# S4D convolution and gated GLU on one core: stores and small scale steps move from ScalarE and VectorE to GpSimd, and the last output stores are cut differently

## The chip, the cores and the metric

The program runs on one core of a Trainium2 chip. The metric is device time in microseconds; lower is better. The engines are called as the profile calls them: PE is TensorE, PEld its weight load, DVE VectorE, ACT ScalarE, POOL GpSimd, and SP SyncE, which only issues DMAs here. A name with a q behind it (ACTq, SPq) is that engine's sequencer, on whose rows the DMA issues of ACT and SP stand.

## What is computed

The input is u, 2048 tokens of 448 channels. With xn the layer norm of u over the channels:

```
out = u + S4D(xn) + GLU(xn)
S4D:  K[d, l] = 2 Re sum_n C[d, n] dt[d] exp(A[d, n] dt[d] l),   256 states n for each of 448 channels d
      y = irfft(rfft(xn, 4096) * rfft(K, 4096))[:2048] + xn * D_skip
GLU:  (sigmoid(xn @ w_gate) * (xn @ w_up)) @ w_down,   448 -> 1792 -> 448
```

All of it is in float32.

## The kernel before

Two generators are interleaved by weights written into the code: `conv()` makes the S4D kernel and the convolution, and `glu()` the gated products. A scheduler then orders each engine's instructions by its own model of the machine, with some priorities and orderings given by hand. Within an engine that order is fixed, and each instruction waits for its operands and its buffers.

**Tokens.** The 2048 tokens are 16 blocks of 128. The first half of the GLU works on blocks 0 to 7 and the second on blocks 8 to 15, each in two tiles of 512 tokens. A product in float32 is made of three matmuls of rounded parts (high times high, low times high, high times low), so weights and activations stand twice, as `wh` and `wl`, `hh` and `hl`, `dh` and `dl`. The gate and up products are L709, the down products L825; DVE adds the latter into `acc` (L830). GpSimd makes `dl` (L786) for the first half.

**Norm.** `x_stats` (L245) gives mean and variance of a block, and `x_scales` (L250) the factor `ys` and the offset `zs` by three Newton steps from an integer guess, on DVE, for four blocks at a time in the first half and for all eight of the second half at once. `x_norm` applies them; for the second half that happens late, at about 270 us.

**First stage of x's transform.** For each pair of blocks, PE multiplies by a table `wx` (L280), ACT copies the result out of PSUM, and it is stored to `x1_d` in DRAM. For the first half `x_spec` (L282) does this at about 41 to 73 us: four calls, each with two of three tiles `x1a`, `x1b`, `x1c` in turn (the trace writes `x1ab` for the first two), PSUM banks `tr`, `ko` and `kp`, copies at L293 and L295, and four stores at L300, issued by ACT. A tile can be written again only when its stores have landed, and a bank only when its copy is done. For the second half `pair_first` (L681) does it at about 273 to 330 us: four calls with four PSUM banks `gu`, copies at L689 and four stores at L691, also issued by ACT. Nothing reads `x1_d` before the spectra, after 510 us.

**S4D kernel.** From about 107 to 510 us GpSimd builds magnitudes `me` and `mf` (L508, L520) for two groups of channels at a time, one pair ahead; DVE multiplies them into `Et` and `Ft` (L602 to L604), and PE sums them (`ko`, L616). GpSimd also adds the skip to `ks` (L627) and, from 332 us, issues loads of weights for the second half (L640 to L648).

**End.** The spectra's last inverse stage (L962) is done in steps `last(h, m)` that add into `acc` tiles for channel half h; those for h = 1 stand between the last four down products (L811 to L818). `out` (L235) stores blocks of tokens in four DMAs, one for each group of 32 partitions. The first channel half of blocks 8 to 11 goes on POOL's queue; the rest of blocks 8 to 11, then blocks 12 to 14, then block 15 go on the queues of SP and ACT in turn.

Of the kernel before, what the change touches and what calls it, by code (L numbers as in the profile page):

```python
# [15 lines left out]
ALU = mybir.AluOpType  # L16
# [4 lines left out]
D = 448  # L21
# [18 lines left out]
H = D // 2  # L40
# [91 lines left out]
def s4d_glu_kernel(ctx, tc, io):  # L132
    nc = tc.nc
    hp = tc.high_priority
    v = nc.vector
# [114 lines left out]
    def x_scales(sm, b0, nb):  # L250

        st6, mv, ve, z = sm
        y = ys[:, b0 : b0 + nb]
        b = slice(b0 % 8, b0 % 8 + nb)
        v.tensor_scalar(ve[:, b], mv[:, b, 1], 1e-5, None, ALU.add)  # L255
        v.tensor_scalar(y.bitcast(I32), ve[:, b].bitcast(I32), -0.5, 1597463007.0, ALU.mult, ALU.add)
        for _ in range(3):
            v.tensor_tensor(z[:, b], y, y, ALU.mult)
            v.scalar_tensor_tensor(z[:, b], z[:, b], -0.5, ve[:, b], ALU.mult, ALU.mult)
            v.scalar_tensor_tensor(y, z[:, b], 1.5, y, ALU.add, ALU.mult)  # L260
        neg = lim[:, b0 // 4, 0:1] if b0 < 8 else -1.0
        v.scalar_tensor_tensor(zs[:, b0 : b0 + nb], mv[:, b, 0], neg, y, ALU.mult, ALU.mult)
        if b0 < 8:
            limits(b0 // 4)

    def x_norm(xn, xt, b):
        y_, z_ = ys[:, b : b + 1], zs[:, b : b + 1]
# [14 lines left out]
    def x_spec(xn, b0):  # L282

        x1s_ = []
        for _ in range(2):
            x1s_.append(slots[("x1a", "x1b", "x1c")[x1s[0] % 3]])
            x1s[0] += 1
        ps = psc[-1].tile([128, 2, 512], F32, name="tr", bufs=1)
        kk = [psc[-1].tile([128, 512], F32, name=n, bufs=1) for n in ("ko", "kp")]
        with tc.issue_after(glu_mm[0].ins):  # L290
            for j in range(4):
                x_first_stage((ps[:, j] if j < 2 else kk[j - 2])[:, :D], xn, j)
        nc.scalar.copy(x1s_[0], ps[:, :, :D])  # L293
        for j in range(2):
            nc.scalar.copy(x1s_[1][:, j], kk[j][:, :D])  # L295
        for p in range(2):
            r = row(b0, 2 * p)
            for h in range(2):
                to = x1_d[h].rearrange("(g r) k d -> g r k d", r=8)[r // 8 : r // 8 + 2, r % 8 : r % 8 + 2]
                nc.scalar.dma_start(to.rearrange("g i k d -> (i k) g d"), x1s_[p][:, :, H * h : H * h + H])  # L300
        yield 2 * WX

    def exp(ex, ki, fr, pl):
# [377 lines left out]
    def pair_first(b, xns):  # L681

        x1 = pg.tile([128, 2, D], F32, name="x1", tag="wraw", bufs=1)
        pss = [psg.tile([128, 512], F32, name="gu", bufs=4) for _ in range(4)]
        for g in range(4):
            x_first_stage(pss[g][:, :D], xns, g)
        for g in range(4):
            to = x1[:, g] if g < 2 else pg.tile([128, D], F32, name="x1", tag="rd", bufs=RB)
            nc.scalar.copy(to, pss[g][:, :D])  # L689
            r = row(b, g)  # L690
            nc.scalar.dma_start(  # L691
                x1_d[:, r : r + 2].rearrange("h i k d -> (i k) h d"), to.rearrange("p (h d) -> p h d", h=2)
            )

# [35 lines left out]
    def glu():  # L730
        for half in range(2):
# [4 lines left out]
            for fs_ in ORDER[half]:  # L736
# [68 lines left out]
                for t in range(2):  # L805
                    acc = accs[2 * half + t]
                    for b in range(4):
                        if final and (t, b) == (0, 1):

                            yield None  # L810
                        if final and t == 1 and b >= 2:  # L811

                            sp_mm[:] = glu_mm
                            for m in (4 * b - 8, 4 * b - 6):
                                lasts[0](1, m)
                            if b == 3:
                                out(accs[2], 8, 4, slice(H, D), (nc.sync, nc.scalar))
                                out(accs[3], 12, 3, slice(0, D), (nc.sync, nc.scalar))  # L818
                        po = psg.tile([128, D], F32, name="po", tag="gu", bufs=4)
                        bs = slice(128 * b, 128 * b + 128)  # L820
                        n = 0
                        with tc.issue_after(sp_mm[0].ins) if glu_on else nullcontext():
                            for (hh, hl), (dh, dl) in zip(hs[t], wts):
                                for a_, w_ in ((hh, dh), (hh, dl), (hl, dh)):
                                    glu_mm[:] = [nc.tensor.matmul(  # L825
                                        po, a_[:, bs], w_, start=(n == 0), stop=(n == 3 * fc - 1)
                                    )]
                                    n += 1
                        with hp(HP):
                            v.scalar_tensor_tensor(  # L830
                                acc[:, b], po, 0.5, acc[:, b], ALU.mult, ALU.add
                            )
                        yield 0.6 * fc
                        if cross and (t, b) in downs:
                            step(*downs[t, b])
# [2 lines left out]
                    if final and t == 0:  # L838
                        out(acc, 8, 4, slice(0, H), (nc.gpsimd,))
                    elif final:  # L840
                        out(acc, 15, 1, slice(0, D), (nc.sync, nc.scalar))

    def spectra(pf):

# [310 lines left out]
```

## Time and profile before

| | us |
|---|---|
| runs | 711.12, 714.69, 714.64 |
| median | 714.64 |
| profiled execution | 710.54 |
| its span, first to last instruction | 708.8 |
| PE busy | 668.1 |
| DVE busy | 555.7 |
| ACT busy | 428.7 |
| POOL busy | 384.9 |
| mean granted clock of TensorE | 0.988 |

The profile is of one execution, which was shorter than the median. DMA issues of ACT and SP are not counted as busy, those of POOL are shown as its own rows. A row of the timeline gives start and duration in us, engine, line, operation, the tiles written and read, and in brackets the idle time of the engine ahead of it with what ended it. Rows of windows give start and end of a stretch, then the busy time of each engine in it, the granted clock (1.00 is full), the share of the DMA engines and GB/s.

### The profile page before, as it was taken

The page shows a single profiled execution, that of the slowest core. Times are in us where ns is not written, and L with a number is a line of the kernel's source. Part 1 is how long each engine was busy: PE and PEld are TensorE (multiplying, and loading weights), DVE is VectorE, ACT ScalarE, POOL GpSimd, SP SyncE. Part 2 cuts the span into 40 slices and gives each one's busy share as a digit, 9 for nine tenths or more (in the row PEclk, how much of TensorE's full clock was granted, in tenths as well). Part 3 has the DMA queues.
Part 4 walks back from the last instruction along what each step waited for, and adds up shares of the span by engine and source line. Part 5 has one row for each costly group of instructions (what it writes and reads, how often), then busy time and mean ns, then how long its engine had stood idle before and what let it go on. Part 6 is the DMA issues. An engine that isn't in the chain of part 4 may idle for free. (4 is left out here: it accounts for less than half of the span.)

```text
span 708.8 us, 19098 instructions
## 1 busy us (share of the span) xinstructions
PE 668.1 (94%) x7752; PEld 523.7 (74%) x7752; DVE 555.7 (78%) x766; ACT 428.7 (60%) x678; POOL 384.9 (54%) x433
## 2 busy tenths in 40 slices
PE   2798999999999998999999999999999999999996
PEld 2575878878877875756878878877777777777784
DVE  5899987699899998898478899988946555566544
ACT  3656965578689779877577788778543322322320
POOL 2101227655999999777446698798765001344001
PEclk9999999999999998989999999999999999999999
DMA  9956274554253544546833333242269988999756
GB/s 200 239 149 204 70 230 150 170 183 132 63 169 135 169 123 135 162 146 202 258 112 103 92 112 108 68 138 82 54 179 280 257 236 238 266 272 221 182 146 182
DMA packets 93031, 117.22 MB, mean 165 GB/s; under 512 B 12240, under 2 KB 76624, under 8 KB 92944
## 3 DMA queue, kind: packets, MB, share of 16 engines
q1 hardware_dynamic: 65376, 91.75, 46.3%
q10 hardware_dynamic: 24896, 18.13, 8.7%
q0 software_dynamic: 2672, 6.13, 3.2%
q8 instruction: 61, 1.00, 0.6%
q14 instruction: 26, 0.21, 0.1%
HBM read 72.13 MB, written 43.84 MB: 164 GB/s over the span
## 5 line engine op out<-in xcount | busy, mean ns | idle before, releaser
L520 POOL TENSOR_TENSOR me<-me,pm 128x32 f32<-128x32 f32 (+1 forms) x168 | 154.9, 922 | 66.8 <-DVE Et L603 38.1
L520 POOL TENSOR_TENSOR mf<-mf,pm 128x64 f32<-128x64 f32 (+1 forms) x112 | 116.9, 1044 | 5.1
L709 PE MATMUL gu<-xh,wh 128*128 128x512 f32 x336 | 100.1, 405 | 3.8 <-DVE acc L830 1.6
L709 PE MATMUL gu<-xh,wl 128*128 128x512 f32 x336 | 96.9, 393 | 0.0
L709 PE MATMUL gu<-xl,wh 128*128 128x512 f32 x336 | 95.1, 390 | 0.0
L602 DVE TENSOR_TENSOR Et<-me,S 128x1024 f32<-128x1024 f32 x56 | 80.2, 1433 | 11.6 <-ACT S L551 10.3
L825 PE MATMUL po<-dh,hh 128*128 128x448 f32 x224 | 84.2, 376 | 3.1 <-ACT hh L725 1.9
L548 ACT ACTIVATE S<-tr 128x1024 f32<-128x1024 f32 x56 | 57.7, 1030 | 44.9 <-PE tr L542 41.0
L604 DVE TENSOR_TENSOR Ft<-mf,S 128x1024 f32<-128x1024 f32 x56 | 80.1, 1431 | 5.3 <-PE ko L616 3.7
L603 DVE TENSOR_TENSOR Et<-me,S 128x1024 f32<-128x1024 f32 x56 | 80.4, 1436 | 4.8 <-ACT me L533 4.5
L825 PE MATMUL po<-dh,hl 128*128 128x448 f32 x224 | 82.4, 369 | 0.3 <-DVE hl L727 0.3
L825 PE MATMUL po<-dl,hh 128*128 128x448 f32 x224 | 82.3, 368 | 0.0
L709 PEld LDWEIGHTS gu<-xh,wh 128*128 128x128 f32 x336 | 60.8, 189 | 24.2 <-issue 4.4
L709 PEld LDWEIGHTS gu<-xh,wl 128*128 128x128 f32 x336 | 63.4, 189 | 14.7 <-DVE ve L255 0.7
L709 PEld LDWEIGHTS gu<-xl,wh 128*128 128x128 f32 x336 | 63.0, 188 | 13.5
L725 ACT CAST hh<-hf 128x512 fp32r<-128x512 f32 x56 | 34.9, 623 | 62.4 <-DVE hf L720 61.4
L616 PEld LDWEIGHTS ko<-Et,Ft 128*32 128x32 f32 x3584 | 54.7, 112 | 24.2 <-issue 13.4
L720 DVE SCALAR_TENSOR_TENSOR hf<-th,gu 128x512 f32<-128x512 f32 x56 | 38.1, 680 | 39.9 <-PE gu L709 35.2
L786 POOL TENSOR_TENSOR dl<-rd,dh 128x448 fp32r<-128x448 f32 x14 | 25.6, 1830 | 78.8 <-ACT dh L785 68.5
L616 PE MATMUL ko<-Et,Ft 128*32 128x64 f32 x3584 | 65.2, 223 | 2.6 <-DVE Ft L604 2.4
L551 ACT ACTIVATE S<-S,hpi 128x1024 f32<-128x1024 f32 x56 | 65.5, 1170 | 0.0
L717 ACT ACTIVATE th<-gu 128x512 f32<-128x512 f32 x56 | 33.5, 599 | 49.4 <-PE gu L709 43.0
(208 smaller groups left out, 1318.0 us busy)
## 6 DMA issues: line engine op xcount, KB each, us to landing
sk_d<-sk ACTq DMA_DIRECT2D x14, 512.0 KB
sx<-x_d SPq DMA_DIRECT2D x32, 224.0 KB
skl<-sk_d SPq DMA_DIRECT2D x16, 448.0 KB
vp<-v_d SPq DMA_DIRECT2D x16, 448.0 KB
v_d<-vt SPq DMA_DIRECT2D x14, 448.0 KB
ph<-ph_d SPq DMA_DIRECT2D x224, 24.0 KB
wt_d<-wh SPq DMA_DIRECT2D x9, 512.0 KB
wt_d<-wl SPq DMA_DIRECT2D x9, 512.0 KB
```

The source lines that it names most:

```text
L520: ins = nc.gpsimd.tensor_tensor(m[:, :, w + a : 2 * w : n], m[:, :, a:w:n], par(base + i).unsqueeze(2).to_broadcast([128, 4 * DC, w // n]) ...
L548: nc.scalar.activation(rows(cs), pv, AF.Abs)
L551: sins[:] = [nc.scalar.activation(cs, cs, AF.Sin, scale=-TWO_PI, bias=hpi)]
L602: v.tensor_tensor(Et[:, :, :, 32:64], two(me[:, :, 32:64]), S[:, 1::-1], ALU.mult)
L603: v.tensor_tensor(Et[:, :, :, 0:32], two(me[:, :, 0:32]), S[:, 1:3, :, ::-1], ALU.mult)
L604: fts[:] = [v.tensor_tensor(Ft, two(mf), S[:, 3:5], ALU.mult)]
L616: mm = nc.tensor.matmul(ko[32 * j : 32 * j + 32, sl], Ft[:, cc, DC * h + 4 * q + j], Et[:, cc, DC * h + 4 * q + j], start=(k == 0), stop=( ...
L709: glu_mm[:] = [nc.tensor.matmul(ps, a_, b_, start=(n == 0), stop=(n == len(mm) - 1))]
L717: marks[0] = nc.scalar.activation(th, pgu[0], AF.Tanh, scale=0.5)
L720: marks[1] = v.scalar_tensor_tensor(hf, th, 1.0, pgu[1], ALU.add, ALU.mult)
L725: nc.scalar.copy(hh, hf)
L825: glu_mm[:] = [nc.tensor.matmul(po, a_[:, bs], w_, start=(n == 0), stop=(n == 3 * fc - 1))]
```

## The change

- The stores of `x_spec` and of `pair_first` are issued by GpSimd and no longer by ACT: 32 DMAs.
- For the second half (`b0 >= 8`) the three Newton steps and `zs` are computed by GpSimd, in 14 instructions of 128x8 in place of ten on DVE, since a step is made of four single operations.
- The last stores are cut differently: the first channel half of blocks 12 and 13 is stored from POOL's queue as soon as block 13's down product is added; at the end SP and ACT store the second channel half of blocks 8 to 11, that of blocks 12 and 13, and then blocks 14 and 15 whole.

```diff
@@ x_scales
+        if b0 >= 8:
+            for _ in range(3):
+                nc.gpsimd.tensor_tensor(z[:, b], y, y, ALU.mult)
+                nc.gpsimd.tensor_tensor(z[:, b], z[:, b], ve[:, b], ALU.mult)
+                nc.gpsimd.tensor_scalar(z[:, b], z[:, b], -0.5, 1.5, ALU.mult, ALU.add)
+                nc.gpsimd.tensor_tensor(y, y, z[:, b], ALU.mult)
+            nc.gpsimd.tensor_tensor(z[:, b], mv[:, b, 0], y, ALU.mult)
+            nc.gpsimd.tensor_scalar(zs[:, b0 : b0 + nb], z[:, b], -1.0, None, ALU.mult)
+            return
         for _ in range(3):
             v.tensor_tensor(z[:, b], y, y, ALU.mult)
             v.scalar_tensor_tensor(z[:, b], z[:, b], -0.5, ve[:, b], ALU.mult, ALU.mult)
             v.scalar_tensor_tensor(y, z[:, b], 1.5, y, ALU.add, ALU.mult)
@@ x_spec
-                nc.scalar.dma_start(to.rearrange("g i k d -> (i k) g d"), x1s_[p][:, :, H * h : H * h + H])
+                nc.gpsimd.dma_start(to.rearrange("g i k d -> (i k) g d"), x1s_[p][:, :, H * h : H * h + H])
@@ pair_first
-            nc.scalar.dma_start(
+            nc.gpsimd.dma_start(
                 x1_d[:, r : r + 2].rearrange("h i k d -> (i k) h d"), to.rearrange("p (h d) -> p h d", h=2)
             )
@@ glu, last down products
                             if b == 3:
                                 out(accs[2], 8, 4, slice(H, D), (nc.sync, nc.scalar))
-                                out(accs[3], 12, 3, slice(0, D), (nc.sync, nc.scalar))
+                                out(accs[3], 12, 2, slice(H, D), (nc.sync, nc.scalar))
...
+                        if final and (t, b) == (1, 1):
+                            out(acc, 12, 2, slice(0, H), (nc.gpsimd,))
...
                     elif final:
-                        out(acc, 15, 1, slice(0, D), (nc.sync, nc.scalar))
+                        out(acc, 14, 2, slice(0, D), (nc.sync, nc.scalar))
```

Since the scheduler orders each engine anew, the change moves instructions beyond those that it names. In the order of the changed program the line numbers are up to nine higher.

On POOL, in the stage of `x_spec`, before: `dl` is the low part of a weight tile of the down product, `pm` a tile of powers.

```order
L1064 DMA sel<-in_c_sel_dram 128x512
L786 TENSOR_TENSOR dl<-rd,dh 128x448 x2
L584 MEMSET pm_1167 128x128
L786 TENSOR_TENSOR dl<-rd,dh 128x448 x2
L477 MEMSET pm_1110 128x128
```

And after, from the same load of `sel` on, as far as the second store of the first `x1c`:

```order
L1073 DMA sel<-in_c_sel_dram 128x512
L793 TENSOR_TENSOR dl<-rd,dh 128x448
L307 DMA x_d<-x1ab 128x2x224 x4
L259 TENSOR_TENSOR z<-ys 128x8
L260 TENSOR_TENSOR z<-z,ve 128x8
L261 TENSOR_SCALAR z<-z 128x8
L262 TENSOR_TENSOR ys<-ys,z 128x8
...
L307 DMA x_d<-x1c 128x2x224 x2
L261 TENSOR_SCALAR z<-z 128x8
L307 DMA x_d<-x1ab 128x2x224 x2
L262 TENSOR_TENSOR ys<-ys,z 128x8
L793 TENSOR_TENSOR dl<-rd,dh 128x448
```

The rows left out are six more Newton rows, so ten stand ahead of the first stores of `x1c`; the last row is the `dl` that started at 54.69 us before, and two stores of `x1ab` and two more Newton rows stand ahead of it as well.

On ACT, in the same stage, before: copies out of PSUM for `x_spec`, stores, and the GLU's `hh`.

```order
L293 COPY x1c<-tr 128x896
L759 CAST wh<-wraw 128x1024
L295 COPY x1ab<-ko 128x448
L373 ACTIVATE s_381<-s_381 112x512
L300 DMA x_d<-x1c 128x2x224 x2
...
L295 COPY x1c<-ko 128x448
L300 DMA x_d<-x1ab 128x2x224 x2
L295 COPY x1c<-kp 128x448
L725 CAST hh<-hf 128x512
```

After:

```order
L300 COPY x1c<-tr 128x896
L766 CAST wh<-wraw 128x1024
L302 COPY x1ab<-ko 128x448
L380 ACTIVATE s_385<-s_385 112x512
...
L302 COPY x1c<-ko 128x448
L302 COPY x1c<-kp 128x448
L732 CAST hh<-hf 128x512
```

The copies keep their places, and the stores between them are gone; the second pair of copies to `x1c` and `hh` behind them now depend on stores in POOL's order.

On DVE, in the stage of `pair_first`, at about 306 to 311 us, before: `xl` is the low part of the normed tokens, read out of the bank that PE's next transposes need.

```order
L720 SCALAR_TENSOR_TENSOR hf<-th,gu 128x512
L269 TENSOR_SCALAR xt<-xt,ys,zs 128x448
L220 TENSOR_TENSOR xl<-gu,xh 128x2x256
L604 TENSOR_TENSOR Ft<-mf_1108,S_1103 128x1024
L454 SCALAR_TENSOR_TENSOR pm_1110<-pm_1110 128x128
L830 SCALAR_TENSOR_TENSOR acc<-po,acc 128x448
L223 TENSOR_TENSOR xl<-gu,xh 128x256
```

After:

```order
L727 SCALAR_TENSOR_TENSOR hf<-th,gu 128x512
L276 TENSOR_SCALAR xt<-xt,ys,zs 128x448
L220 TENSOR_TENSOR xl<-gu,xh 128x2x256
L611 TENSOR_TENSOR Ft<-mf_1112,S_1107 128x1024
L461 SCALAR_TENSOR_TENSOR pm_1114<-pm_1114 128x128
L223 TENSOR_TENSOR xl<-gu,xh 128x256
L837 SCALAR_TENSOR_TENSOR acc<-po,acc 128x448
```

`acc` and the second `xl` have changed places. In the same stage POOL's 16 stores stand among its magnitudes: four ahead of the second pair of groups in that stage, four ahead of the third, four within it or at its end, and four within the fourth, ahead of the loads of L640.

More of the change, by code (lines that the diff above doesn't have):

```diff
@@ L260, in x_scales @@
             v.scalar_tensor_tensor(y, z[:, b], 1.5, y, ALU.add, ALU.mult)
[L261 to L264, printed above, removed]
+        v.scalar_tensor_tensor(zs[:, b0 : b0 + nb], mv[:, b, 0], lim[:, b0 // 4, 0:1], y, ALU.mult, ALU.mult)
+        limits(b0 // 4)
     def x_norm(xn, xt, b):
```

## The prediction

> **What bounds the kernel now.** I read the busy shares and the clock row of the page first, then the chain that ended last, then what TensorE (PE) waited for, stage by stage.
>
> ```profile
> PE 668.1 (94%) x7752; PEld 523.7 (74%) x7752; DVE 555.7 (78%) x766; ACT 428.7 (60%) x678; POOL 384.9 (54%) x433
> ...
> PEclk9999999999999998989999999999999999999999
> ```
>
> PE is busy 94% of the span of 708.8 us, so some 41 us at most are not matmuls. ScalarE (ACT), from which work is taken, is busy only 60%. The clock row is full but for two slices at about 270 to 320 us. The chain of work that ended last shows the tail:
>
> ```profile
> 694.71 1.67 PE pv L962 x64
> ...
> 700.08 2.03 PE po L825 x9
> 702.10 0.02 issue
> 702.12 0.62 DVE acc L830
> ```
>
> The chain is PE almost throughout; the last sum of VectorE (DVE) ends at 702.74, and the remaining 6.06 us are output stores. Where PE did wait in the stages that the change touches, its timeline says (start, duration, what; in brackets the idle time ahead and its releaser):
>
> ```profile
> 61.25 0.47 PE L825 MATMUL po<-dh,hh 128*128 128x448 f32 x1 [1.85 <-ACT hh L725]
> ...
> 69.41 0.47 PE L825 MATMUL po<-dh,hh 128*128 128x448 f32 x1 [1.20 <-DVE acc L830]
> ...
> 305.91 1.99 PE L280 MATMUL gu<-xt,wx 32*64 32x448 f32 x8 [0.92 <-DVE hf L720]
> ...
> 309.89 0.56 PE L213 MATMUL gu<-ident,xt 128*64 128x128 f32 x2 [0.77 <-DVE xl L223]
> ```
>
> These waits name DVE, or ACT's hh that itself waited for DVE's hf (its row is below). No wait names an issue of a store. Behind the gaps near 270 to 310 us lies a second price, in the windows (length, then busy time and count of PE, PEld, DVE, ACT, POOL, then granted clock, DMA share, GB/s):
>
> ```profile
> 270.00:280.00 10.00, 8.00 (x96) 4.20 (x94) 10.00 (x12) 9.54 (x17) 9.61 (x9) 0.96 0.34 95
> 280.00:290.00 10.00, 10.00 (x150) 6.93 (x149) 6.28 (x7) 8.24 (x14) 8.67 (x12) 0.69 0.51 160
> 300.00:310.00 10.00, 8.26 (x120) 4.90 (x119) 9.52 (x13) 7.59 (x14) 9.28 (x13) 1.00 0.50 162
> 310.00:320.00 10.00, 10.00 (x122) 6.74 (x122) 9.61 (x11) 8.83 (x15) 4.96 (x6) 0.66 0.35 110
> ```
>
> After a window in which PE was busy 8.00 of 10 (and again 8.26), the granted clock falls: 0.04, 0.31 and 0.34 of 10 us are lost, 0.4 + 3.1 = 3.5 us and 3.4 us. So one such stretch is worth up to 3.5 us of PE.
>
> **The change part by part.**
>
> *Stores of the first stage leave ACT.* Sixteen are issued at 43 to 73 us and sixteen at 278 to 330 us. What one cost ACT is read from what ACT starts beside it:
>
> ```profile
> 43.22 0.40 ACTq L300 DMA_DIRECT2D x_d<-x1ab  x1
> 43.29 0.64 ACT L725 CAST hh<-hf 128x512 fp32r<-128x512 f32 x1
> ...
> 55.45 1.92 ACTq L300 DMA_DIRECT2D x_d<-x1ab  x2
> ...
> 57.41 0.53 ACT L295 COPY x1c<-kp 128x448 f32<-128x448 f32 x1 [1.56 <-PE gu L709]
> ...
> 60.58 0.62 ACT L725 CAST hh<-hf 128x512 fp32r<-128x512 f32 x1 [2.64 <-DVE hf L720]
> ...
> 301.98 2.77 ACTq L691 DMA_DIRECT2D x_d<-x  x2
> 304.79 0.58 ACT L219 CAST xh<-gu 128x512 fp32r<-128x512 f32 x1 [2.41 <-issue]
> ```
>
> hh starts 0.07 us after an issue of 0.40 began: an issue normally costs ACT nothing, since it runs beside computing. Twice it did not: ACT stood still for 1.56 us before 57.41 (the row names PE, but the gap ends with the issue, at 57.37) and for 2.41 us before 304.79. Both were covered: after the first, ACT waited another 2.64 us for hf; during the second DVE worked on. So 3.97 us of ACT go, and the path gets **0**; what is late next is DVE in both places.
>
> *The same stores on GpSimd (POOL).* The trace has no such store there; the nearest issues are these, with the landing times of the output stores:
>
> ```profile
> L239 POOL DMA_DIRECT2D out_dram<-ac x8 | 4.4, 554 | 0.1
> L640 POOL DMA_DIRECT2D wraw<-in_B_w_up_dram x5 | 3.9, 778 | 0.0
> ...
> DMA to landing us min/median/max: 2.4/2.7/6.9
> ```
>
> So 0.55 to 0.78 us each (the mean ns of the rows); a store of 128x2x224 lies between these shapes, and I take 0.6. In the second stage 16 x 0.6 = 9.6 us (8.8 to 12.5) come onto POOL in front of the magnitudes. The cover is POOL's own waiting for DVE to release a buffer of me:
>
> ```profile
> 292.64 6.69 POOL L520 TENSOR_TENSOR me<-me,pm 128x32 f32<-128x32 f32 x6 [3.73 <-DVE Et L603]
> ...
> 319.79 4.59 POOL L520 TENSOR_TENSOR me<-me,pm 128x32 f32<-128x32 f32 x6 [4.73 <-DVE Et L603]
> ```
>
> The order puts four stores ahead of the first wait (2.4 us against 3.73) and eight between the two (4.8 against 4.73): just covered, and the magnitudes are made one pair of groups ahead of their use. I take **0**; if the cover were gone, the end would slip by the excess, at most 12.5 - 8.46 = 4.0 us.
>
> *Newton steps.* Ten rows leave DVE. Their cost there is the spacing of starts:
>
> ```profile
> 47.38 0.17 DVE L256 TENSOR_SCALAR ys<-ve 128x8 int32<-128x8 int32 x1
> ...
> 53.54 0.16 DVE L258 TENSOR_TENSOR z<-ys 128x8 f32<-128x8 f32 x1
> 53.62 1.76 DVE L322 RECIPROCAL m<-m 112x128 f32<-112x128 f32 x2
> ...
> 68.74 0.62 DVE L830 SCALAR_TENSOR_TENSOR acc<-po,acc 128x448 f32<-128x448 f32 x1
> ```
>
> 53.62 - 53.54 = 0.08 us each, 0.8 in all; five stand ahead of the acc at 68.74 on which PE waits: 0.4 us earlier. On POOL they become 14 instructions. The nearest shape is ks (128x8), and beside it stands what POOL and DVE do to each other:
>
> ```profile
> L627 POOL TENSOR_TENSOR ks<-ks,dm x14: 215/654/1192, 163.5 to 524.8; 128x8 f32<-128x8 f32 x14
> ...
> 36.44 1.15 POOL L786 TENSOR_TENSOR dl<-rd,dh 128x448 fp32r<-128x448 f32 x1 [11.26 <-ACT dh L785]
> ...
> 84.11 4.41 POOL L786 TENSOR_TENSOR dl<-rd,dh 128x448 fp32r<-128x448 f32 x1 [24.74 <-ACT dh L785]
> ...
> 88.02 1.05 DVE L392 SCALAR_TENSOR_TENSOR w<-ci,w 112x512 f32<-112x512 f32 x1
> ```
>
> The same dl took 1.15 us at 36 us and 4.41 at 84 us, inside a dense run of DVE; at its end the DVE instruction at 88.02 took 1.05, where its neighbours start 0.60 apart: POOL waited for DVE, then DVE 0.4 for POOL. So the 14 steps cost POOL 3.0 to 16.7 us, 9.2 at the median, and give DVE back at least one such wait of 0.4 because dl moves behind them. I put the Newton part at -0.4 + 0.4 = **0** on the path, with -0.4 to +3 as its bounds (14 short waits of 0.2).
>
> Queued behind them are two stores of x1c, the third dl and the next stores; this is the wait that the change adds. Ten steps stand ahead of the x1c stores. From 47.55 (ys ready): 10 x 0.65 = 6.5, two issues 1.2, landing 2.7 give **57.95**; only then may ACT overwrite x1c (two copies, 1.1 us, before: 55.29 and 57.41) and go on to hh. That makes 59.05, ahead of the 60.58 at which hh starts anyway. Covered by 1.5 us.
>
> The Trainium skill, "SBUF — State Buffer", section "Who interferes with whom", says that a DVE instruction with two SBUF inputs and a GpSimd one that reads SBUF exclude each other for a whole instruction. The 4.41 us row agrees with it. By that rule alone the steps come late and in lumps, and the time is that of the second rival below; by the median of the ks row it is the sum's. The same page's section "SBUF: two separate sides" adds that GpSimd's own DMA descriptors can be locked out by some DVE modes; no row here shows that.
>
> *The tail.* The last stores, by queue (KB each):
>
> ```profile
> out_dram<-acc SPq DMA_DIRECT2D x2, 168.0 KB
> ...
> out_dram<-acc SPq DMA_DIRECT2D x2, 112.0 KB
> ...
> out_dram<-acc SPq DMA_DIRECT2D x2, 56.0 KB
> ...
> 703.00:704.00 1.00, 0.00 (x0) 0.00 (x0) 0.00 (x0) 0.00 (x0) 0.00 (x0) 1.00 1.05 325
> ```
>
> Before: 2 x (112 + 168 + 56) = 672 KB on SP's queue and as much on ACT's; after: 2 x (56 + 112 + 112) = 560. 224 KB leave the tail for POOL's queue, some 8 us earlier. After the last sum the DMA engines are full (share 1.05 at 325 GB/s), so the end follows the bytes: 224 / 325 = **0.7 us** less. The bounds are 0 (if the last 448 KB, now twice those before, set the end by their own issue) and -1.2 (if also 0.5 us of earlier start counts).
>
> *Sum.* 0 + 0 + 0 - 0.7 = -0.7 us. Against the profiled execution's own 710.54 us that is 709.8. That execution is 4.1 us under the median of the runs shown, 714.64; these lie at 711.12 and at 714.64 to 714.69, which is one clock stretch of 3.5 apart (an inference: only one run has a profile). The change decides nothing about that that I can price, so the forecast for the median is 714.64 - 0.7 = **713.9 us**.
>
> **The rivals.** *One clock stretch fewer.* In the order, xl now stands ahead of acc:
>
> ```profile
> 308.90 0.61 DVE L830 SCALAR_TENSOR_TENSOR acc<-po,acc 128x448 f32<-128x448 f32 x1
> 309.43 0.41 DVE L223 TENSOR_TENSOR xl<-gu,xh 128x256 fp32r<-128x256 f32 x1
> ```
>
> That takes 0.5 us of PE's 0.77 wait at 309.89, right ahead of the drop of the clock. If it is enough, 3.4 us go: 713.9 - 3.4 = **710.5**. Against it: the gaps at 273 to 278 us stay, and it is a threshold that I cannot see. The same time comes out if the median run just falls into the faster group.
>
> *The stores of x1c come late.* At 1.19 us a step, the most for that shape, ten steps end at 59.45, the stores are issued by 60.65 and land at 63.35; ACT's copies end at 64.45, hh at 65.1, and PE goes on at about 65.1 and not 61.25: 3.8 us, of which the later 1.2 us wait gives back that much: 2.6. A gap of PE of that length would bring a clock stretch of 3.4 too: 713.9 + 6.0 = **719.9**, slower than before. It decides from landings later than 59.5 us. For it speaks the 4.41 us row; against it that DVE's reciprocals at 53.6 to 57.5 have one input.
>
> **How the numbers follow.** A measurement of this kernel tells about 0.5% (3.6 us) from no change. Forecast 713.9, within 0.5%: 0.42. Fewer stretches, or the faster group, at 710.5 and faster by over 0.5%: 0.36. Late stores, or POOL's cover gone by the full 4.0 us with a stretch: 0.22. The range reaches from 709.0 (710.5 less the tail's other 0.5 and a further 1) to 718.0 (713.9 and the 4.0 us); left out is most of the late-store case.
>
> **What would show it.** In the changed profile: the ACT stalls at 55 and 302 us are gone and no PE wait with them; the x1c stores on POOL start before 55 us and ACT's second copy to x1c ends by 60.5; POOL's waits for Et shrink to near 0 but PE never names POOL's me; DMA is idle after the last sum 0.7 us sooner. I am wrong if PE waits longer than 2 us at 58 to 66 us, if the count of windows below full clock changes, or if the last store ends later against the last sum than the 6.06 us of before.

## The result, and the profile after

| | median, us | runs | ratio to before on the same chip | 95% interval |
|---|---|---|---|---|
| before | 712.79 | 5 | | |
| after | 723.13 | 5 | 1.0153 | 1.0124 to 1.0183 |
| after, measured once more beside the experiments | 726.50 | 5 | 1.0169 | 1.0148 to 1.0191 |

The forecast was 713.9 us, 709.0 to 718.0: no change. The kernel became 1.5 to 1.7% slower, 10 to 12 us. The profiled execution took 722.0 us, with a span of 720.2, against 710.54 and 708.8.

The page, read at the same two lines as before:

```profile
PE 675.9 (94%) x7752; PEld 529.3 (73%) x7752; DVE 560.7 (78%) x756; ACT 428.2 (59%) x678; POOL 415.6 (58%) x483
...
PEclk9999999999999999979899999999999999999999
```

The shares say almost nothing: PE is again at 94%, and POOL has 30.7 us more to do but is still idle 42% of the time. PE's waits say more (who waited for whom: total, times, longest). Before, the longest wait for Ft was 0.7 us:

```profile
PE ko L616 <- DVE Ft L604: 2.4, 5, 0.7
...
PE po L825 <- DVE acc L830: 1.2, 1, 1.2
```

After:

```profile
PE ko L623 <- DVE Ft L611: 10.2, 4, 6.7
PE po L832 <- DVE acc L837: 3.3, 1, 3.3
```

In PE's timeline after, the wait of 1.85 us at 61.25 is gone (between 58 and 70 us PE now waits at most 0.48). The wait of 1.20 us for acc at 69.41 has grown to 3.26, and the wait of 6.70 is new:

```profile
72.29 0.47 PE L832 MATMUL po<-dh,hh 128*128 128x448 f32 x1 [3.26 <-DVE acc L837]
...
359.19 1.93 PE L623 MATMUL ko<-Et,Ft 128*32 128x64 f32 x64 [6.70 <-DVE Ft L611]
```

The windows after show what lies behind such gaps:

```profile
310.00:320.00 10.00, 9.09 (x89) 4.46 (x86) 9.94 (x15) 6.94 (x13) 9.56 (x12) 0.58 0.36 114
...
350.00:360.00 10.00, 3.30 (x43) 2.52 (x46) 2.70 (x3) 1.45 (x2) 0.91 (x2) 0.80 0.77 247
360.00:370.00 10.00, 10.00 (x182) 7.99 (x178) 7.87 (x10) 5.32 (x9) 5.42 (x9) 0.86 0.53 136
```

The first row answers to before's 0.66 in the same window. From 350 to 370 us the clock was full before (1.00 in both windows). Now PE loses 6.70 us there to the wait and about 1.8 us to the clock behind it. The two windows together lose 0.20 + 0.14 of 10 us, 3.4 us of clock, but 1.6 of these fall into the wait itself, where PE had nothing to run: in windows of 2 us the clock is 0.51 from 356, 0.50 from 358 and from 360, and 0.79 from 362. Where the time goes is best read from one mark that both programs have in the same order, DVE's 56 instructions Ft. Their start after, less that before, in the profiled executions (us; the column heads are times of before):

```
                                   120.3  278.8  330.4  342.3  381.6  519.9  end of span
after                                2.5    4.1    4.2   15.6   12.5   12.5   11.4
after, second profile                3.4    5.5    5.2   15.6   13.2   13.3   13.2
before with the new tail only        0.3    0.2    2.8    2.8    2.9    3.1    6.5
```

There are two losses: 2.5 to 3.4 us before 120 us, and 8 us between 330 and 380 us. The last row is a warning: that program has the order of before up to its last stores, so its drift of 2.8 us at 320 us and of 3 more behind 520 us is the scatter between executions. Single traces show mechanisms; sizes are taken from the ratios of the runs.

**The loss in the middle is a chain over four queues.** After, on POOL: the last of `pair_first`'s stores stand between steps of `mf`.

```profile
336.06 3.44 POOL L527 TENSOR_TENSOR mf<-mf,pm 128x64 f32<-128x64 f32 x3
339.44 0.75 POOL L698 DMA_DIRECT2D x_d<-x  x1
340.21 1.08 POOL L527 TENSOR_TENSOR mf<-mf,pm 128x512 f32<-128x512 f32 x1
341.21 1.47 POOL L698 DMA_DIRECT2D x_d<-x  x2
```

On SP, after: the load of `t` (the spectra's table t32, not read before 510 us) reuses a tile that these stores read. It stood at the head of SP's queue, and what it waited for stands in SP's own waits:

```profile
SPq L986 <- DMA x_d<-x: 9.9, 1, 9.9
```

```profile
344.02 0.36 SPq L986 DMA_DIRECT2D t<-in_c_t_dram  x1
...
347.24 0.54 SPq L846 DMA_DIRECT2D acc_d<-acc  x1
347.87 8.95 SPq L499 DMA_DIRECT2D ph<-ph_d  x8
```

Before, the same rows of SP came some 10 us earlier, and the next phase loads 12.9 us behind the store:

```profile
333.17 0.36 SPq L977 DMA_DIRECT2D t<-in_c_t_dram  x1
...
337.75 0.38 SPq L837 DMA_DIRECT2D acc_d<-acc  x1
...
350.68 6.10 SPq L492 DMA_DIRECT2D ph<-ph_d  x8
```

The last sum for this store ended at 335.90 before and at 340.71 after. So of the 11.4 us by which the load of `acc` below starts later (344.86 and 356.24), 4.8 are lateness that the program already had, 4.7 were added by SP's queue ahead of the store, and 1.9 passed between the store and the load (7.1 us before, 9.0 after).

The store of `acc` (the finished sums of tokens 512 to 1023) must land before `acc`'s buffer is loaded anew, and that load is issued by ACT (L243). Here the scheduler's new order matters. On ACT before, the four loads followed `hh`; after, one of them stands ahead of it:

```profile
343.28 0.62 ACT L724 ACTIVATE th<-gu 128x512 f32<-128x512 f32 x1
356.24 0.32 ACTq L243 DMA_DIRECT2D acc<-in_A_u_dram  x1
356.65 0.62 ACT L732 CAST hh<-hf 128x512 fp32r<-128x512 f32 x1 [12.75 <-DMA ph<-ph_d]
```

ACT stood still for 12.75 us with `hf` ready since 345.45, and so did DVE, with `hl` and then `Ft` behind it:

```profile
344.76 0.69 DVE L727 SCALAR_TENSOR_TENSOR hf<-th,gu 128x512 f32<-128x512 f32 x1 [4.05 <-PE gu L716]
357.30 0.69 DVE L734 TENSOR_TENSOR hl<-hf,hh 128x512 fp32r<-128x512 f32 x1 [11.85 <-ACT hh L732]
357.91 1.22 DVE L611 TENSOR_TENSOR Ft<-mf,S 128x1024 f32<-128x1024 f32 x1
```

The row of `hh` names the phase loads, which share SP's queue with the store; that it is the store which ACT waits for is an inference from the buffer that the load writes, and the experiments below bear it out. Before, `hh` ran first and the loads could wait as long as they liked; the `th` behind them waited 5.75 us, with no wait of PE:

```profile
341.03 0.62 ACT L725 CAST hh<-hf 128x512 fp32r<-128x512 f32 x1 [1.03 <-DVE hf L720]
344.86 2.45 ACTq L243 DMA_DIRECT2D acc<-in_A_u_dram  x4
347.40 0.60 ACT L717 ACTIVATE th<-gu 128x512 f32<-128x512 f32 x1 [5.75 <-DMA acc<-in_A_u_dram]
```

**The early loss is a chain too.** Before, POOL made the third `dl` as soon as ACT had made `dh`, and the load of the next `rd` followed on SP:

```profile
54.69 2.23 POOL L786 TENSOR_TENSOR dl<-rd,dh 128x448 fp32r<-128x448 f32 x1 [17.09 <-ACT dh L785]
```

```profile
56.95 0.35 SPq L648 DMA_DIRECT2D rd<-in_B_w_down_dram  x1
```

After, twelve Newton instructions and eight stores stand on POOL between the second `dl` and the third:

```profile
48.00 0.65 POOL L259 TENSOR_TENSOR z<-ys 128x8 f32<-128x8 f32 x1
...
53.53 1.49 POOL L307 DMA_DIRECT2D x_d<-x1c  x2
...
58.50 1.58 POOL L793 TENSOR_TENSOR dl<-rd,dh 128x448 fp32r<-128x448 f32 x1
```

So `dl` began 3.8 us later. It frees the tile `rd`; the load of the next `rd` heads SP's queue and went out 3.2 us later, with the loads of `wraw` behind it. ACT's `wh` waits for these loads:

```profile
60.11 0.35 SPq L655 DMA_DIRECT2D rd<-in_B_w_down_dram  x1
```

```profile
68.80 1.04 ACT L766 CAST wh<-wraw 128x1024 fp32r<-128x1024 f32 x1 [2.05 <-DMA wraw<-in_B_w_up_dram]
```

The new order has this `wh` ahead of `hh` on ACT, and `wl` ahead of the `acc` on DVE that PE waited 3.26 us for. Before, `hh` stood first:

```profile
66.82 0.62 ACT L725 CAST hh<-hf 128x512 fp32r<-128x512 f32 x1
...
67.96 1.03 ACT L759 CAST wh<-wraw 128x1024 fp32r<-128x1024 f32 x1
```

### The profile page after: what moved, and what is told of

Same layout as the page of the kernel before. It is cut to its first block, busy times and chain, and to the rows that moved or that the text cites. A ratio compares the mean times of both kernels' runs of the same rounds, so it can differ in the third digit from the quotient of the medians.

```text
span 720.2 us, 19137 instructions
## 1 busy us (share of the span) xinstructions
PE 675.9 (94%) x7752; PEld 529.3 (73%) x7752; DVE 560.7 (78%) x756; ACT 428.2 (59%) x678; POOL 415.6 (58%) x483
## 4 chain that ended last, share of the span: by engine, by line
PE 68%; DVE 17%; DMA 5%; ACT 3%; issue 3%; SPq 3%; POOL 1%; ACTq 0%; DVEq 0%; POOLq 0%
PE gu L716 30%; PE po L832 14%; PE sp L911 7%; PE ko L623 5%; PE pv L938 4%; PE tr L549 3%; DVE Ft L611 3%; DVE Et L609 3%; DVE Et L610 2%; DMA acc<-in_A_u_dram 1%; DMA acc_d<-acc 1%; DVE acc L837 1%; PE pv L971 1%; SPq L649 1%; DVE hl L734 1%
## 5 line engine op out<-in xcount | busy, mean ns | idle before, releaser
L527 POOL TENSOR_TENSOR mf<-mf,pm 128x64 f32<-128x64 f32 (+1 forms) x112 | 114.0, 1018 | 5.1
L716 PE MATMUL gu<-xl,wh 128*128 128x512 f32 x336 | 96.6, 394 | 0.0
L609 DVE TENSOR_TENSOR Et<-me,S 128x1024 f32<-128x1024 f32 x56 | 84.1, 1503 | 10.5 <-ACT S L558 9.4
L611 DVE TENSOR_TENSOR Ft<-mf,S 128x1024 f32<-128x1024 f32 x56 | 81.6, 1456 | 4.6 <-PE ko L623 3.2
L610 DVE TENSOR_TENSOR Et<-me,S 128x1024 f32<-128x1024 f32 x56 | 79.6, 1422 | 5.1 <-ACT me L540 4.5
L623 PEld LDWEIGHTS ko<-Et,Ft 128*32 128x32 f32 x3584 | 56.2, 114 | 32.2 <-DVE Ft L611 12.9
L623 PE MATMUL ko<-Et,Ft 128*32 128x64 f32 x3584 | 66.8, 228 | 11.2 <-DVE Ft L611 10.2
L734 DVE TENSOR_TENSOR hl<-hf,hh 128x512 fp32r<-128x512 f32 x56 | 45.5, 813 | 25.6 <-ACT hh L732 25.6
L837 DVE SCALAR_TENSOR_TENSOR acc<-po,acc 128x448 f32<-128x448 f32 x80 | 48.2, 616 | 18.8 <-PE po L832 18.8
```

What stands on the lines that cost most here:

```text
L527: ins = nc.gpsimd.tensor_tensor(m[:, :, w + a : 2 * w : n], m[:, :, a:w:n], par(base + i).unsqueeze(2).to_broadcast([128, 4 * DC, w // n]) ...
L609: v.tensor_tensor(Et[:, :, :, 32:64], two(me[:, :, 32:64]), S[:, 1::-1], ALU.mult)
L610: v.tensor_tensor(Et[:, :, :, 0:32], two(me[:, :, 0:32]), S[:, 1:3, :, ::-1], ALU.mult)
L611: fts[:] = [v.tensor_tensor(Ft, two(mf), S[:, 3:5], ALU.mult)]
L623: mm = nc.tensor.matmul(ko[32 * j : 32 * j + 32, sl], Ft[:, cc, DC * h + 4 * q + j], Et[:, cc, DC * h + 4 * q + j], start=(k == 0), stop=( ...
L716: glu_mm[:] = [nc.tensor.matmul(ps, a_, b_, start=(n == 0), stop=(n == len(mm) - 1))]
```

## The experiments

The theories, by the letters that the expectations use. W: the load of `acc` ahead of `hh` makes the loss in the middle. C is W with its whole chain: the load's place and the late store of `acc` together make it. E: the early loss comes from Newton steps and stores together in front of `dl` and of `x1c`'s stores. The rivals: P and S, the added work on POOL costs time by itself; O, the new order costs it, however early the store of `acc` lands. Every ratio is to the kernel before on the same chip, with its 95% interval. The diffs of 1 and 3 are against the kernel before, the others against the changed kernel.

**1. The parts alone: Newton steps, `x_spec`'s stores, `pair_first`'s stores, tail.** Each applies one part of the change and nothing else; the Newton steps and the tail as in the diff above, the stores by a word each.

```diff
@@ x_spec (second kernel)
-                nc.scalar.dma_start(to.rearrange("g i k d -> (i k) g d"), x1s_[p][:, :, H * h : H * h + H])
+                nc.gpsimd.dma_start(to.rearrange("g i k d -> (i k) g d"), x1s_[p][:, :, H * h : H * h + H])
@@ pair_first (third kernel)
-            nc.scalar.dma_start(
+            nc.gpsimd.dma_start(
```

Newton steps alone: 

> The kernel before with the Newton steps of the second half on GpSimd and nothing else: no store moves to POOL. In the order two loads of an acc tile now stand ahead of the first hh of the second half on ACT. Theory W: the wait comes although no store has moved: 4 to 10 us slower than before, 717 to 723, with PE waiting for Ft at about 340 to 360 us. Theory P: 14 small steps on POOL, 3 to 9 us of it at 48 us where POOL has room: within 2 us of before.

`x_spec`'s stores alone: 

> The kernel before with x_spec's 16 stores on POOL and nothing else. PE's order is that of before. Theory E (the early loss of 3 to 5 us needs both the stores and the Newton steps on POOL: together they put dl, and with it SP's load of rd and the loads of wraw behind that, 3 us late): within 1.5 us of before, 711.5 to 714. Rival S (the stores alone cost it, six of them at 0.75 us stand ahead of dl): 715 to 718.

`pair_first`'s stores alone: 

> The kernel before with pair_first's 16 stores on POOL and nothing else. In the order one load of acc stands ahead of hh and t's load ahead of the second store of acc, as in the changed kernel. Theory C: the whole middle loss comes from this part: PE waits 4 to 7 us for Ft at about 350 us, 718 to 721. Rival: the middle loss needs the 3 us that the changed kernel is already late at 115 us, or the Newton steps' order: then 712 to 715.

The tail alone: 

> The kernel before with the new cut of the last stores and nothing else; every engine's order is that of before up to the last stores. Both theories: the last store ends 4.9 us after the last sum, as in the changed kernel, and not 6.06: 1.1 us faster than before (0.7 by the prediction's bytes). If the tail gives nothing, the same time as before.

| part alone | median, us | before, us | ratio | 95% interval |
|---|---|---|---|---|
| Newton steps | 715.32 | 712.70 | 1.0014 | 0.9983 to 1.0045 |
| `x_spec`'s stores | 713.42 | 712.26 | 1.0008 | 0.9983 to 1.0033 |
| `pair_first`'s stores | 719.02 | 712.26 | 1.0089 | 1.0063 to 1.0115 |
| tail | 713.63 | 712.70 | 0.9991 | 0.9963 to 1.0019 |

Only `pair_first`'s stores cost time alone, 0.9%, in the middle of the kernel, as theory C has it; in that profile PE waited 3.08 us for Ft at 354.33, less than the 4 to 7 expected. The sum is 1.4 + 0.8 + 8.9 - 0.9 = 10.2 thousandths, the whole change 15.3 to 16.9. So about 5 to 7 would be made only by parts together, but the four intervals add up to some 6 thousandths either way, and these runs alone do not settle it; experiment 6 does. The tail's expected 1.1 us is too small for these intervals. My expectation for the Newton steps alone (717 to 723) was wrong, and usefully: in that program two loads of `acc` stand ahead of `hh` too, and ACT waited, but the store of `acc` went out at 344.50, 2.0 us behind the last sum, the load could start at 350.42, and between 334 and 362 us PE waited once, 0.61 us, and not for Ft. The order alone does not make the loss.

**2. The load of `acc` behind `hh` again.** In the diffs of 2 and 3 `hhs` lists the casts to `hh` and `lds` the loads of tokens; most lines that fill them are left out.

```diff
-                    x_load(accs[q], 4 * q, 4, [nc.scalar])
+                    if q == 2:
+                        x_load(accs[q], 4 * q, 4, [nc.scalar])
...
+                    if half == 1 and (f, t) == (f0, 0) and fs_ is ORDER[1][0]:
+                        with tc.issue_after(hhs[-1].ins):
+                            x_load(accs[3], 12, 4, [nc.scalar])
```

> The changed kernel with one thing put back: the load of the fourth acc tile is issued behind the first hh of the second half, as before the change. Nothing else in any engine's order changes. Theory W (that load, which waits on ACT for the landing of the store of acc, holds hh back, and hl, Ft and PE behind it): PE's wait of 6.70 us at 359 goes, and with it most of the clock that was lost behind it (0.20 and 0.14 of 10 us, 3.4 us): 723.1 - 6.7 - 3.4 = 713.0, at most 716.4 if the clock part stays. Theory P (the 32 stores and the Newton steps cost what they take of POOL, 0.75 us a store, and push the whole middle back): the wait is only shifted, 720 to 723.

Measured: 720.57 us against 712.70, ratio 1.0090 [1.0056, 1.0124]. PE's wait is gone. `hh` starts when `hf` is done, though the loads come as late as in the changed kernel:

```profile
349.08 0.62 ACT L734 CAST hh<-hf 128x512 fp32r<-128x512 f32 x1 [2.64 <-DVE hf L729]
355.84 1.73 ACTq L243 DMA_DIRECT2D acc<-in_A_u_dram  x4
```

Between 330.4 and 381.6 the mark slips by 1.0 us (6.5 to 7.5) and not by 8.3. So the place of this one DMA is worth 6 to 8 thousandths, some 4.5 to 5.6 us, together with the late store; each of the two ratios behind such a difference has an interval of about 3 thousandths either way. The early loss was there in full (3.6 us at 120 us, 6.1 at 279), which is why the time did not fall to the 713.0 to 716.4 that W, as the only cause, gave. The time lies in the range of P, but what P said does not hold: the wait was not shifted, it is gone.

**3. The same load ahead of `hh` in the kernel before.** The mirror of 2; before's stores stay on ACT.

```diff
-        with hp(HP):
-            nc.scalar.copy(hh, hf)
+        with hp(HP), tc.issue_after(lds[-4].ins) if len(accs) == 4 and not hhs else nullcontext():
+            one_ = nc.scalar.copy(hh, hf)
```

> The kernel before with one load of acc put ahead of the first hh of the second half on ACT, as the changed kernel has it; on DVE hl moves behind Ft and Et of the same step, no other order changes. Theory C (the place of the load costs nothing by itself: it decides only with a store of acc that lands late; before the change it landed at 344.86, and hh's result is next needed after 348): within 2 us of before, 711 to 715. Theory O (the place alone): 717 to 721 with PE waiting 4 us or more at 345 to 360 us.

Measured: 713.26 against 711.84, ratio 0.9996 [0.9971, 1.0020]. ACT waited, but only until 343.46, and PE did not wait once between 335 and 362 us (at 334.58 it waited 1.81 us for `acc`, where before had 0.70):

```profile
343.46 0.32 ACTq L245 DMA_DIRECT2D acc<-in_A_u_dram  x1
343.82 0.63 ACT L729 CAST hh<-hf 128x512 fp32r<-128x512 f32 x1 [4.31 <-DMA acc_d<-acc]
```

This row names the store of `acc` as the releaser. Theory O falls: the place costs nothing where the store lands in time. (`hl` stands behind `Ft` in this program, which helps it too.)

**4. SP's load of `t` behind the store of `acc`.** Only SP's order changes.

```diff
-                        nc.sync.dma_start(acc_d[:, 4 * t : 4 * t + 4], acc)
+                        kept_[:] = [nc.sync.dma_start(acc_d[:, 4 * t : 4 * t + 4], acc)]
...
-        nc.sync.dma_start(t32, io["c_t32"])
+        with tc.issue_after(kept_[0].ins) if kept_ else nullcontext():
+            nc.sync.dma_start(t32, io["c_t32"])
```

> The changed kernel with one move on SP's queue: the load of t (t32, not read before 510 us) is issued behind the second store of acc and not ahead of it; no other engine's order changes, and the load of acc stays ahead of hh on ACT. Theory C (a chain: pair_first's last stores go out late behind POOL's magnitudes, their landing at 344.0 lets SP issue t's load, which reuses a tile they read, and only behind it comes the store of acc at 347.2, whose landing ACT's load ahead of hh needs): the store of acc goes out at about 341 to 344, hh comes before PE needs it, PE's 6.70 us wait goes or is under 2: 723.1 - 6.7 = 716.4, and 713.0 with the clock behind it. Theory O (the place of the load ahead of hh is enough, whenever the store of acc goes out): 721 to 723.

Measured: 719.83 against 712.26, ratio 1.0094 [1.0067, 1.0122], between the 716.4 of C and the 721 to 723 of O. The store went out at 344.82, in a program that ran 3.7 us later than the after of the first profile at 330 us (7.9 against 4.2). That is 0.4 us behind the last sum, against 6.5 in that profile. PE's wait of 6.70 is gone, and the mark slips by 1.4 us in place of 8.3:

```profile
344.82 0.44 SPq L848 DMA_DIRECT2D acc_d<-acc  x1
```

```profile
353.88 0.32 ACTq L243 DMA_DIRECT2D acc<-in_A_u_dram  x1
354.30 0.62 ACT L732 CAST hh<-hf 128x512 fp32r<-128x512 f32 x1 [6.66 <-DMA sk_d<-sk]
```

The load is still ahead of `hh`; it no longer hurts. Either link of the chain, cut alone, gives back 6 to 8 thousandths (2 and 4).

**5. Newton steps back on DVE, with the `t` of 4.** The diffs of the Newton steps undone and of 4.

> The changed kernel with the Newton steps back on DVE and t's load behind the second store of acc; all 32 stores stay on POOL, and the tail stays changed. Theories C and E: both losses are gone, the tail's 1.1 us stays: 711 to 713. If the stores' 24 us on POOL cost time by themselves: 716 to 720.

Measured: 716.24 against 712.26, ratio 1.0043 [1.0018, 1.0067]: short of the expected 711 to 713, and in the range that stores costing time by themselves would give (experiment 8 comes back to this). The store left at 338.58, yet the load behind it started only at 350.62:

```profile
338.58 0.38 SPq L841 DMA_DIRECT2D acc_d<-acc  x1
342.17 0.33 SPq L982 DMA_DIRECT2D t<-in_c_t_dram  x1
342.60 8.34 SPq L492 DMA_DIRECT2D ph<-ph_d  x8
```

```profile
353.60 1.73 PE L616 MATMUL ko<-Et,Ft 128*32 128x64 f32 x64 [3.12 <-DVE Ft L604]
```

12.0 us from store to load, against 7.1 before. In this trace the DMA engines are full from 338 to 348 us (shares of 0.90 to 1.09), with the phase loads close behind the store on SP and POOL's loads of `wraw` at 340 to 344; before, they were full from 336 to 344 as well. What stretched this landing was not tested. One thing can be counted: from this store to the load it took 5.9 to 7.1 us in the traces of the seven kernels with `pair_first`'s stores on ACT, and 8.5 to 12.0 in those of the eight with them on POOL. The load's place ahead of `hh` stays a risk.

**6. The Newton steps on POOL, but late.** They stay on POOL behind the early stores and `dl`; nothing needs them before 270 us.

```diff
-                x_scales(sm, 8, 8)
...
-        nc.gpsimd.memset(pms[0][:, 6], 1.0)
+        with tc.issue_after(nc.gpsimd.memset(pms[0][:, 6], 1.0).ins):
+            x_scales(sm, 8, 8)
```

> The changed kernel with the Newton steps still on POOL, but behind the stores of x_spec and the first dl tiles (their results are not needed before 270 us). All other engines keep the changed kernel's order but for two rows of PE. Theory E (the early loss comes from Newton steps that stand ahead of x1c's stores and of dl and are slow while DVE is busy): the early loss is that of the stores alone, 0.6 us at 120 us and not 2.5 to 6.4: 723.1 less 2 to 6, so 717 to 721; the 6.7 us wait at 350 to 360 us stays. Rival: the early loss comes from the other engines' new order (wh and wl ahead of hh and acc): 722 to 724.

Measured: 720.97 against 714.28, ratio 1.0100 [1.0080, 1.0120], while the changed kernel beside it had 1.0169: 5 to 7 thousandths come from where the Newton steps stand. The other engines keep the new order (`wh` ahead of `hh`), so the order alone is not the cause, and the rival falls. `dl` starts at 55.33, `rd` is loaded at 56.86 and no longer 60.11:

```profile
55.33 1.50 POOL L794 TENSOR_TENSOR dl<-rd,dh 128x448 fp32r<-128x448 f32 x1
```

```profile
56.86 0.35 SPq L656 DMA_DIRECT2D rd<-in_B_w_down_dram  x1
```

The wait in the middle is there as expected (7.06 us at 356.65).

The late load alone is not the cause either. With the Newton steps alone (1) `dl` began at 60.77 and `rd`'s load went out at 61.93, later than in the changed kernel; but that program has the order of before, `hh` ahead of `wh`, and the `acc` that PE waits for began at 69.83, against 68.74 before, 71.62 in the changed kernel and 69.48 here. With `x_spec`'s stores alone the order is the new one, and the load is early (57.15): `acc` began at 69.45. So the Newton steps bring the late load, `x_spec`'s stores bring the order, and the early loss needs both. This corrects E, which had both only in front of `dl`.

**7. Both cut.** The diffs of 2 and 6; and, without the Newton steps on POOL, the diffs of 2 and of the Newton steps undone.

> The last kernel with the load of the fourth acc tile behind the first hh of the second half as well; all four parts of the change are in it. Theories W and E together: both losses gone, the tail's 1.1 us stays: 711 to 714. If half of the 10 us has another cause: 716 to 718.

> The changed kernel with the Newton steps back on DVE and the load of the fourth acc tile behind hh; all 32 stores stay on POOL, the tail stays changed. Theories W and E: 711 to 714. If the stores on POOL cost time by what POOL does later (the magnitudes), whatever stands ahead of hh: 716 to 718, with PE waiting for Et or Ft at 300 to 360 us.

Measured: 716.30 and 716.18 against 714.28, ratios 1.0047 [1.0024, 1.0069] and 1.0032 [1.0013, 1.0051]. Of 15 to 17 thousandths 11 to 14 are gone, and 2.3 to 3.4 us are left, more than the expected 711 to 714; 716 to 718 was what the rivals gave. In the second of them PE waits three times for ACT's copies of `pair_first`, 1.02, 0.25 and 0.24 us; the second of these copies had itself waited 1.62 us for a store's landing. The first wait:

```profile
327.88 0.47 PE L831 MATMUL po<-dh,hh 128*128 128x448 f32 x1 [1.02 <-ACT x L689]
```

**8. Is the rest `pair_first`'s stores?** First only the stores of `pair_first` back on ACT, then these back on ACT and the Newton steps late as in 6.

```diff
@@ pair_first
-            nc.gpsimd.dma_start(
+            nc.scalar.dma_start(
```

> The changed kernel with the 16 stores of pair_first back on ACT; the stores of x_spec, the Newton steps and the tail stay changed. In the order all loads of acc stand behind hh again. Theory W: no wait for Ft at 340 to 360 us; what is left against before is what the earlier stage costs (PE waits of 3.3 us for acc and a clock of 0.83 at 70 to 80 us) less 1.1 us at the tail: 711 to 716. Theory P: the second 16 stores are about half of POOL's added 30 us, so about half of the 10.3 us lost goes: 717 to 719.

> The changed kernel with pair_first's stores back on ACT and the Newton steps on POOL behind the early stores; x_spec's 16 stores and the Newton steps stay on POOL and the tail stays changed. If the 2.3 to 3.3 us that are left with both waits mended belong to pair_first's stores (PE's three waits for ACT's copies into tiles whose stores have not landed, 1.5 us, and what follows): 711 to 713. If they belong to x_spec's stores, the Newton steps or the new order: 715 to 717.

Measured: 716.57 against 712.70, ratio 1.0046 [1.0017, 1.0076], just above W's 711 to 716; and 712.79 against 711.84, ratio 1.0009 [0.9983, 1.0035]. With the pair's stores on ACT the mark hardly moves between 330.4 and 381.6 (6.0 and 6.0; 0.7 and 1.2). So what is left in 7 belongs to `pair_first`'s stores, 4.7 - 0.9 = 3.8 thousandths, with an interval of about 3.4 either way; `x_spec`'s 16 stores, the late Newton steps and the new tail then cost nothing that can be measured. By which of PE's waits or clock stretches these stores cost the 3.8, or whether it is POOL's time that does, stays open.

The first of these two kernels also caught the early loss at its worst. On POOL, and on DVE at the same time:

```profile
48.26 5.54 POOL L259 TENSOR_TENSOR z<-ys 128x8 f32<-128x8 f32 x1
...
59.31 1.49 POOL L307 DMA_DIRECT2D x_d<-x1c  x2
```

```profile
48.16 0.69 DVE L374 SCALAR_TENSOR_TENSOR m<-a,b 112x512 f32<-112x512 f32 x1
...
53.66 1.76 DVE L329 RECIPROCAL m<-m 112x128 f32<-112x128 f32 x2
```

One step of 128x8 took 5.54 us, through ten DVE instructions: it ended when DVE's dense run, begun at 48.16, came to its first reciprocal. The same step took 0.65 us after. The stores of `x1c` came 5.8 us later than after, ACT's copy waited 5.87 us for them, and PE waited:

```profile
63.40 1.01 PE L287 MATMUL ko<-xn,wx 32*64 32x448 f32 x2 [2.80 <-ACT x1c L302]
```

The same 5.54 us stand in the trace of 4, at 47.98, and with the Newton steps alone (1) their third step took 5.48; in both profiles of the changed kernel the step took 0.64 or 0.65.

**9. The changed kernel again.** 

> The changed kernel once more, on the chip of these runs, for its second profile: 722 to 725 or 1.012 to 1.018 of before. The wait for Ft at 350 to 360 us is there again (5 us or more); the early loss at 120 us may be 2.5 us as in the first profile or 6 us as in the two experiments where x1c's stores came later.

Measured: 726.50 against 714.28, as the table above has it; a wait of 4.70 us for Ft at 359.14, a little under the 5 expected, and 3.65 us for acc at 73.27.

Eight traces now have a load of `acc` ahead of `hh`. Put side by side, the time from the last sum of `acc` to that load goes with PE's longest wait for Ft behind it (us):

| trace | last sum to load | PE's wait for Ft |
|---|---|---|
| load ahead of `hh` in the kernel before (3) | 7.9 | 0 |
| Newton steps alone (1) | 7.9 | 0 |
| `t` behind (4) | 9.4 | 0.8 |
| `pair_first`'s stores alone (1) | 12.3 | 3.1 |
| Newton steps on DVE, `t` behind (5) | 12.8 | 3.1 |
| changed kernel, second profile | 14.1 | 4.7 |
| changed kernel, first profile | 15.5 | 6.7 |
| Newton steps late (6) | 15.8 | 7.1 |

Before, with the load behind `hh`, it was 9.0. So some 9 us are covered in this kernel, and what is more goes to PE nearly in full (15.5 less 9.0 is 6.5, where PE waited 6.7).

No version here beats the kernel before by a measurable amount; the new tail alone, and `x_spec`'s stores with late Newton steps and the new tail, equal it.

## Why the prediction was wrong, step by step

- **"The same stores on GpSimd ... just covered ... I take 0" is the step that failed.** It asked only whether POOL's magnitudes come late. They did not: POOL's waits for Et shrank from 3.73 and 4.73 to 2.29 and 0, as foreseen, and PE never named `me`. It did not ask who waits for the stores to land. The prediction worked the landing out for `x1c`, which ACT writes again; but the tiles that `pair_first`'s stores read are freed at the landing too, and SP's load of `t` and ACT's next copies wait for that. Measured: 0.9% with this part alone, 6.3 us of 712.26.
- **"What is late next is DVE in both places"** held at 55 us. In the middle what was late next was the store of `acc`, through a load that the scheduler had put ahead of `hh`. The order on ACT at that place was not compared, since the step asked only about the rows near the moved stores.
- **The price of an issue, 0.6 us, was too low:** 0.72 to 0.80 us each, 23.6 us for 32, and POOL's busy time grew by 30.7 us with the Newton steps. By itself that size decided nothing.
- **"Newton ... 0", with -0.4 to +3 as bounds,** is the second failure. Alone it is 1.4 thousandths, unresolved; with `x_spec`'s stores, and the order that they bring, it is 5 to 7 (experiment 6). The text named "the third dl" as queued behind the steps, and stopped there: `dl` frees `rd`, and SP's queue holds `wraw` behind `rd`'s load. The ten steps ended at 53.6 in the profile, sooner than the 54.05 forecast (47.55 + 6.5), and in another execution at 59.4, against 59.45 in the rival with 1.19 us a step.
- **The rival "the stores of x1c come late"** was right in mechanism, and happened in two of the traces (2.80 us of PE at 63 us, where 3.8 were worked out). In both profiles of the changed kernel it did not: the copies waited 2.5 to 2.7 us, and `hh` waited for `hf` anyway. The 719.9 that it gave was the nearest of the forecasts, but by luck: the loss has another reason.
- **The tail** went as worked out. The last sum ends at 715.30 and the span at 720.2:

```profile
714.68 0.62 DVE L837 SCALAR_TENSOR_TENSOR acc<-po,acc 128x448 f32<-128x448 f32 x1 [0.50 <-PE po L832]
```

  4.90 us in place of 6.06, so 1.16 less, within the bounds of 0 to 1.2 and above the 0.7 taken; the second profile has 5.47 and the tail alone 5.16, so 0.6 and 0.9 less. In the runs it is below what can be measured.
- **"One clock stretch fewer"** did not come: windows of 10 us below 0.95 of full clock went from two to eight, two of them at the new wait. But the profile of the new tail alone, with the order of before up to its last stores, has six: such a count from single executions is a poor sign.
- **The signs of being wrong** did not look where the loss was. PE waited at most 0.48 us at 58 to 66 us and the last store ended sooner against the last sum; of the three only the clock count changed, and the waits of 3.26 and 6.70 us stood at 72 and 359 us.

The Trainium skill, "SBUF — State Buffer", section "Who interferes with whom", says that a DVE instruction with two SBUF inputs and a GpSimd one that reads SBUF shut each other out for a whole instruction. The 5.54 us row, which ends with DVE's last two-input instruction of the run, agrees that POOL is shut out, but it lasted for ten DVE instructions of 0.42 to 0.69 us, and two of these (L398) have one SBUF input; the 0.65 us row in the same run of DVE shows that POOL can also get in between them. The rule gives the danger, not the price.

## What to carry to other kernels

A store that is moved to another queue also moves the moment at which its source tile is free: list who reuses that tile, on which in-order queue that instruction stands, and what stands behind it there. When a scheduler orders the engines anew, compare the whole order for DMAs that wait (a load into a buffer still being stored) and now stand ahead of an instruction on the critical path; such a place costs nothing while the landing is in time (up to some 9 us behind the last sum here), and then PE pays for the lateness. An engine's idle share is no cover for work that others wait for in order.

## What the runs showed of the hardware that was not expected

- A POOL step of 128x8 beside the same DVE instructions took 0.2 to 0.65 us in some executions and 5.48 or 5.54 in others.
- From the issue of a store of 896 KB on SP to the first load into its buffer it took 5.9 to 12.0 us, and 8.5 or more whenever `pair_first`'s stores were POOL's.
- The granted clock fell to 0.50 behind two idle times of PE of only 0.75 and 1.25 us (before, 280 to 286 us). Behind the wait of 6.70 us it was 0.5 already 3 us before the wait ended, and for 3.7 us after it.
